# A branch gated on the last store but one, and ten small VectorE writes in an early wait

## The chip, the cores and the metric

The kernel runs on one core of one Trainium2 chip. The metric is the device time of one execution in microseconds, the median of several runs of the same program. A separate execution was recorded by the hardware profiler; all rows shown come from it. The core has five engines, each with its own queue of instructions: TensorE (PE; its weight loads are listed as PEld), VectorE (DVE), ScalarE (ACT), GpSimd (POOL) and SyncE (SP), which here only issues transfers and waits. A letter q behind the name (DVEq, SPq) stands for what the engine's sequencer does itself: waits on semaphores, branches, issue of transfers.

## The reference

Two stages over 4 batches, 8 heads, 768 positions, head width 64, in 8 blocks of 96 positions:

```
P = sort_net                                  # 4 x 8 x 8 x 8
5 times: P = exp(P - max(P, row)); P = P / rowsum; P = P / columnsum
k_sorted, v_sorted = P mixes the 8 blocks of k and of v
scores = scale * q_block @ k_sorted_block^T   # inside each block of 96
attn   = exp(scores - max) / sum ;  x = attn @ v_sorted
wq, wk = x @ w_q, x @ w_k
mixed  = (scale * wq @ wk^T) @ x
out    = relu(mixed) @ w_out                  # 4 x 768 x 512, float32
```

## The kernel before

Everything for the four batches is unrolled into one straight program. Its order is written out by hand in the string ORDER: each item is a unit (a letter for the kind, the batch, a number) with the engine or the PSUM bank that it uses, and the units are recorded in that order on the engines' queues. An engine executes its queue strictly in order.

At the start SyncE loads the sort matrix into `Pm` (L105). VectorE zeroes a padding column and the tile `fil` (L170, L171), then waits for the sort matrix and, with ScalarE for the exponentials, works through the five normalisations (`u_a` and `u_c`, L166 to L185). Meanwhile TensorE multiplies `fil` with itself 40 times, GpSimd prepares constants (`u_i`, with an affine select on `Lx` at L196) and issues the loads of q, k and v. From the sorted weights VectorE and GpSimd make the mixing matrices `M` (L234), and TensorE starts on the batches: sorting of k and v, transposes, scores, exponentials, products, and the second stage, all through the helper at L150 (matmul) and the copies at L154 (ScalarE) and L156 (VectorE).

The exponentials are taken without subtracting a maximum. GpSimd therefore tests all reciprocal sums (`test`, L457 to L461) and writes a flag `bad`; each of GpSimd, ScalarE, TensorE and VectorE loads it into a register (`flag`, L464). At the end of the program a branch on that register (L497) either enters a slow repair of the whole computation, some 450 instructions on VectorE, or jumps over it to the common end. With the inputs here it is always jumped over. Branch hints for TensorE and VectorE (`hint`) announce that the jump is likely. 

The outputs go through four buffers `ot` of two tiles each. For the last batch every tile of 128 rows is stored by a transfer of its own (`u_y`, L446), in the order 0, 1, 3, 4, 5, 2: tile 5 is the last but one, tile 2 the last. Buffer and half of a tile are given by `oslot`.

Ahead of the branch stands a gate (L492 to L496). VectorE writes one element into each half of the three buffers that the last batch uses; each such write has to wait until the stores out of that buffer have landed. Then VectorE writes `past`, and a tiny product on TensorE and a tiny copy on ScalarE read it, so that neither reaches its branch ahead of the gate. Behind the branch each engine raises a closing semaphore (L497). SyncE, which doesn't branch, goes through its closing waits (L598) one after the other: first the transfers, among them the last two stores in order, then the closing semaphores of VectorE, TensorE and ScalarE together with older transfers; then drains and a barrier of all engines end the program.

Of the kernel before, what the change touches and what calls it, by code (L numbers as in the profile page):

```python
# [56 lines left out]
def kernel(  # L57
# [11 lines left out]
    nc = tc.nc  # L69
# [18 lines left out]
    LAST = B - 1  # L88
# [9 lines left out]
    def tiles(name, n, shape, dtype=BF16):  # L98
        return [sb.tile(shape, dtype, name=f"{name}{i}") for i in range(n)]
# [23 lines left out]
    NOT = 4  # L123
    ot = tiles("ot", NOT, [P, 2, DM], FP32)
# [12 lines left out]
    past = sb.tile([1, 4], BF16, name="past")  # L137
# [5 lines left out]
    def rows(t):  # L143
        return t.unsqueeze(2).to_broadcast([BH, NB, NB])

    def cols(t):
        return t.unsqueeze(1).to_broadcast([BH, NB, NB])
# [20 lines left out]
    def u_c(b, n, e):  # L168
        if n == 0:
            nc.vector.memset(Pm[:, NB:NB + 1, :], 1e-9)  # L170
            nc.vector.memset(fil, 0.0)  # L171
            nc.vector.reduce_max(tmp, Pv, axis=AX.X)
            nc.vector.tensor_sub(Pv, Pv, rows(tmp))
            return
        nc.vector.reduce_sum(tmp, Pv, axis=AX.X)
        nc.vector.reciprocal(tmp, tmp)
        nc.vector.tensor_mul(Pv, Pv, rows(tmp))
        nc.vector.reduce_sum(tmp, Pm.rearrange("p i j -> p j i"), axis=AX.X)
        nc.vector.reciprocal(tmp, tmp)
        if n < 5:  # L180
            nc.vector.tensor_mul(Pv, Pv, cols(tmp))
            return
        nc.vector.tensor_mul(Pb.rearrange("p (i j) -> p i j", j=NB), Pv, cols(tmp))
        for a in range(2):
            nc.vector.transpose(PbT[:, a, :], Pb[:, a * BH:(a + 1) * BH])  # L185
# [249 lines left out]
    def oslot(b, n):  # L435
        return ot[(b * 3 + n // 2) % NOT][:, n % 2, :]
# [36 lines left out]
    for item in ORDER.split():  # L473
# [6 lines left out]
        kind, b, n, arg = UNIT.match(item).groups()  # L480
# [8 lines left out]
            fns[kind](b, num, arg)  # L489


    for n in range(3):  # L492
        nc.vector.memset(ot[(LAST * 3 + n) % NOT][0:1, :, 0:1], 0.0)  # L493
    nc.vector.memset(past[:, 0:1], 0.0)
    mm(PS[0:1, 0, 0:1], past[:, 0:1], past[:, 0:1])
    nc.scalar.copy(past[:, 1:2], past[:, 0:1])  # L496
# [106 lines left out]
```

## Time and profile before

| | |
|---|---|
| median of 3 runs | 107.63 us (107.57 to 107.66) |
| profiled execution, its own time | 107.97 us |
| its span, first to last instruction | 106.1 us |
| granted clock of TensorE | 0.998 |
| busy: PE, DVE, ACT, POOL | 93.6, 74.3, 70.1, 31.2 us |
| last store issued, landed | 101.14, 104.05 us |
| chain: PE, ACT, issue, DVE, DMA | 80%, 6%, 5%, 3%, 3% |

The profiled execution takes 1.9 us beside its span. Times in the rows count from the first instruction. A row of a timeline gives start, length, engine, line, operation, tiles and shapes, and in brackets how long the engine had been idle and what ended that. A row for one source line gives the smallest, median and largest duration in ns, then the first and the last start in us. A row of waits names who waited for whom: sum in us, count, longest. In the DMA view "q14 instruction" and "q8 instruction" are transfers that load instructions, not data (packets, MB, share of 16 engines over the window asked for).

### The profile page before, as it was taken

The page shows a single profiled execution, that of the slowest core. Times are in us where ns is not written, and L with a number is a line of the kernel's source. Part 1 is how long each engine was busy: PE and PEld are TensorE (multiplying, and loading weights), DVE is VectorE, ACT ScalarE, POOL GpSimd, SP SyncE. Part 2 cuts the span into 40 slices and gives each one's busy share as a digit, 9 for nine tenths or more (in the row PEclk, how much of TensorE's full clock was granted, in tenths as well). Part 3 has the DMA queues.
Part 4 walks back from the last instruction along what each step waited for, and adds up shares of the span by engine and source line. Part 5 has one row for each costly group of instructions (what it writes and reads, how often), then busy time and mean ns, then how long its engine had stood idle before and what let it go on. Part 6 is the DMA issues. An engine that isn't in the chain of part 4 may idle for free.

```text
span 106.1 us, 3639 instructions
## 1 busy us (share of the span) xinstructions
PE 93.6 (88%) x1550; PEld 65.7 (62%) x1557; DVE 74.3 (70%) x148; ACT 70.1 (66%) x102; POOL 31.2 (29%) x51
## 2 busy tenths in 40 slices
PE   5999999497897979899999999999999999999800
PEld 1334489485776866678968967686667556444400
DVE  1687789098895795788889887999777755637200
ACT  4101179769786879899779798689835447675510
POOL 5999099999237600000000000000059000000000
PEclk9999999999999999999999999999999999999999
DMA  0899999999999999999985474200039345198880
GB/s 3 84 203 203 203 204 208 200 204 205 206 203 204 190 202 204 204 204 205 207 163 134 115 208 106 76 6 0 0 120 380 139 198 204 60 402 326 296 302 14
DMA packets 18499, 18.55 MB, mean 175 GB/s; under 512 B 1840, under 2 KB 16560, under 8 KB 18480
## 3 DMA queue, kind: packets, MB, share of 16 engines
q0 software_dynamic: 14064, 10.09, 63.4%
q1 hardware_dynamic: 4416, 8.19, 22.1%
q8 instruction: 13, 0.21, 0.8%
q14 instruction: 6, 0.05, 0.1%
HBM read 20.19 MB, written 6.29 MB: 250 GB/s over the span
## 4 chain that ended last, share of the span: by engine, by line
PE 80%; ACT 6%; issue 5%; DVE 3%; DMA 3%; DVEq 0%; ACTq 0%
PE ps L150 80%; ACT E L340 3%; DMA out_dram<-ot 3%; DVE X L365 1%; ACT Vs L154 1%; DVE KT L156 1%; ACT XT L154 1%; ACT QT L154 1%; ACT ot L154 1%; DVE M L234 0%; DVE wk L156 0%; DVE fil L171 0%; DVE RS L363 0%; ACT past L496 0%; DVE ot L493 0%
## 5 line engine op out<-in xcount | busy, mean ns | idle before, releaser
L340 ACT ACTIVATE E<-ps 96x960 bf16<-96x960 f32 (+1 forms) x28 | 24.6, 906 | 3.1 <-PE ps L150 2.7
L150 PE MATMUL ps<-wo,mixT 128*128 128x512 bf16 (+1 forms) x93 | 22.2, 370 | 0.5 <-issue 0.2
L365 DVE TENSOR_TENSOR X<-ps,RS 96x896 bf16<-96x896 f32 (+1 forms) x20 | 20.1, 1007 | 0.7
L150 PEld LDWEIGHTS <-mixT 128*128 128x128 bf16 x100 | 8.9, 98 | 8.6 <-issue 0.2
L154 ACT COPY ot<-ps 128x512 f32<-128x512 f32 (+1 forms) x16 | 8.7, 560 | 8.1 <-PE ps L150 5.8
L457 POOL TENSOR_SCALAR ok<-RS 96x280 bf16<-96x280 f32 x1 | 0.9, 923 | 41.8 <-DVE RS L363 41.8
L150 PE MATMUL ps<-fil 128*128 128x512 bf16 x40 | 11.4, 458 | 1.3 <-DVE fil L171 1.3
L150 PE MATMUL ps<-VT,E 96*128 96x65 bf16 x256 | 11.2, 194 | 1.0 <-issue 0.6
L150 PEld LDWEIGHTS <-E 96*128 96x128 bf16 x256 | 9.8, 97 | 3.3 <-issue 1.1
L150 PE MATMUL ps<-QT,KT 64*128 64x96 bf16 x256 | 9.9, 204 | 1.7 <-issue 1.4
L234 POOL TENSOR_TENSOR M<-PTR,m_p 128x256 bf16<-128x256 bf16 x12 | 8.7, 744 | 7.0 <-PE ps L150 3.9
L156 DVE COPY ot<-ps 128x512 f32<-128x512 f32 x9 | 6.1, 690 | 6.5 <-PE ps L150 3.6
L150 PEld LDWEIGHTS <-KT 64*128 64x128 bf16 x256 | 6.9, 94 | 4.4 <-issue 3.2
L150 PEld LDWEIGHTS <-fil 128*128 128x128 bf16 x40 | 4.5, 115 | 7.8 <-issue 3.5
L154 ACT CAST KT<-ps 128x768 bf16<-128x768 f32 x10 | 7.7, 806 | 1.6 <-PE ps L150 1.5
L150 PE MATMUL ps<-idb,X 96*128 96x96 bf16 x128 | 7.5, 206 | 0.6 <-issue 0.6
L150 PE MATMUL ps<-M,Kn 128*64 128x128 bf16 x192 | 7.5, 221 | 0.3 <-issue 0.3
L156 DVE COPY QT<-ps 128x768 bf16<-128x768 bf16 x13 | 6.7, 550 | 1.5 <-PE ps L150 1.1
L426 ACT ACTIVATE mixT<-ps 128x1024 bf16<-128x1024 f32 x7 | 7.0, 1026 | 0.9 <-PE ps L150 0.6
L150 PEld LDWEIGHTS <-X 96*128 96x128 bf16 x128 | 6.2, 98 | 1.9 <-issue 0.9
L156 DVE COPY VT<-ps 96x1024 bf16<-96x1024 bf16 x7 | 4.8, 687 | 3.6 <-PE ps L150 2.9
L154 ACT COPY XT<-ps 128x768 bf16<-128x768 bf16 x6 | 4.8, 798 | 3.6 <-PE ps L150 3.6
(83 smaller groups left out, 156.8 us busy)
## 6 DMA issues: line engine op xcount, KB each, us to landing
out_dram<-ot SPq DMA_DIRECT2D x9, 512.0 KB, 2.8
Kn<-in_k_dram POOLq DMA_DIRECT2D x4, 768.0 KB, 13.1
Vn<-in_v_dram POOLq DMA_DIRECT2D x4, 768.0 KB, 15.2
Qn<-in_q_dram POOLq DMA_DIRECT2D x4, 768.0 KB, 15.3
VT<-Vs SPq DMA_DIRECT2D x12, 130.0 KB, 2.8
out_dram<-ot SPq DMA_DIRECT2D x6, 256.0 KB, 2.9
wo<-in_moe_w_out_dram POOLq DMA_DIRECT2D x1, 512.0 KB, 22.5
qD<-qkT SPq DMA_DIRECT2D x6, 48.0 KB, 2.7
```

Source lines behind the costliest of these rows:

```text
L150: nc.tensor.matmul(o, w, x, is_transpose=t, start=start, stop=stop, skip_group_check=True)
L154: nc.scalar.copy(o, i)
L156: nc.vector.tensor_copy(o, i)
L234: ENG[e].tensor_tensor(out=M[b % 2][:, h0:h1], in0=src[:, h0:h1].unsqueeze(2).to_broadcast([P, 2, SP, NB]), in1=m_p.unsqueeze(1).unsqueeze ...
L340: nc.scalar.activation(E[b % 2][:, n, 0:2 * w * BLK].rearrange("p (t a c) -> p a t c", a=2, c=BLK), PS[0:BLK, bank:bank + 2, 0:w * BLK].re ...
L365: nc.vector.tensor_mul(xo.rearrange("p (a t d) -> p a t d", a=2, d=D), ps[:, :, :, 0:D], rs.unsqueeze(3).to_broadcast([BLK, 2, w, D]))
L426: nc.scalar.activation(o, i, ACT.Relu)
L457: nc.gpsimd.tensor_scalar(out=okf, in0=rsf, scalar1=1e-30, scalar2=None, op0=ALU.is_ge)
```

## The change

Two edits. Ahead of the branch, one write replaces three: only the half buffer of tile 5 of the last batch (`oslot(LAST, 5)`) is written, so the gate waits for one store, the last but one. SyncE's closing waits are as before, so the program still ends only when all stores have landed. And in `u_c`, between the zeroing of `fil` and the first maximum over the sort matrix, VectorE writes the four elements of `past` ten times, each write behind the one before.

```diff
@@ u_c
         if n == 0:
             nc.vector.memset(Pm[:, NB:NB + 1, :], 1e-9)
             nc.vector.memset(fil, 0.0)
+            for _ in range(10):
+                nc.vector.memset(past, 0.0)
             nc.vector.reduce_max(tmp, Pv, axis=AX.X)
             nc.vector.tensor_sub(Pv, Pv, rows(tmp))
             return
@@ ahead of the branch
-    for n in range(3):
-        nc.vector.memset(ot[(LAST * 3 + n) % NOT][0:1, :, 0:1], 0.0)
+    nc.vector.memset(oslot(LAST, 5)[0:1, 0:1], 0.0)
     nc.vector.memset(past[:, 0:1], 0.0)
     mm(PS[0:1, 0, 0:1], past[:, 0:1], past[:, 0:1])
     nc.scalar.copy(past[:, 1:2], past[:, 0:1])
```

In the stream of VectorE's instructions the ten writes add ten places at the head. At the gate two writes and three separate waits go, five places. The other engines' streams keep their instructions and their order.

## The prediction

> **What bounds the kernel now.** I read the page's chain first, then the chain over the last six microseconds, then what SyncE's queue waits for there, then its final waits one by one.
>
> ```profile
> PE 80%; ACT 6%; issue 5%; DVE 3%; DMA 3%; DVEq 0%; ACTq 0%
> ...
> 100.52 0.59 ACT ot L154
> ...
> 101.14 2.92 DMA out_dram<-ot
> 104.05 0.03 issue
> 104.08 0.02 DVEq L493
> ...
> 104.52 0.19 ACT past L496
> ```
>
> Columns of the lower lines: start, length, what. TensorE sets the pace for 80% of the span, but it ends at about 100.5 us. Then the last copy and the last store (tile 2 of the last batch, lands at 104.05) run alone, and the gate at L493 starts only when that store has landed. The change touches this tail and the wait of VectorE at the very start, nothing between.
>
> ```profile
> SPq L598 <- DMA out_dram<-ot: 2.3, 2, 1.7
> SPq L598 <- DVEq L497: 0.8, 1, 0.8
> L598 SPq EVENT_SEMAPHORE  x1: 28/28/28, 103.5 to 103.5; - x1
> L598 SPq EVENT_SEMAPHORE  x4: 28/28/28, 104.1 to 104.2; - x4
> L598 SPq EVENT_SEMAPHORE  x1: 756/756/756, 104.3 to 104.3; - x1
> L598 SPq EVENT_SEMAPHORE  x2: 28/28/28, 105.1 to 105.2; - x2
> L598 SPq DRAIN  x2: 7/7/7, 105.2 to 105.3; - x2
> ```
>
> These are SyncE's closing waits, in order (length in ns, start in us). The one at 103.5 is freed by the last store but one (after 1.7 us of waiting), the next by the last store (after 2.3 - 1.7 = 0.6 us more). Four short ones follow, then one at 104.3 that lasts 756 ns instead of 28: it waits for VectorE's closing semaphore behind the branch, L497. Only then come two more waits, two drains and the common barrier to 106.1. So after the last store has landed, the way gate, branch, closing semaphore is the longer one, by 756 - 28 = 728 ns.
>
> ```profile
> 100.71 0.06 DVE L493 MEMSET ot<- 1x2 f32 x1 [0.80 <-DMA out_dram<-ot]
> 104.26 0.19 DVE L493 MEMSET ot<- 1x2 f32 x2 [3.49 <-DMA out_dram<-ot]
> 104.43 0.06 DVE L494 MEMSET past<- 1x1 bf16 x1
> L497 DVEq EVENT_SEMAPHORE  x1: 21/21/21, 105.0 to 105.0; - x1
> L497 ACTq EVENT_SEMAPHORE  x1: 17/17/17, 105.0 to 105.0; - x1
> L497 PEldq EVENT_SEMAPHORE  x1: 51/51/51, 105.0 to 105.0; - x1
> ```
>
> The three gate writes, the write of `past` that TensorE and ScalarE wait for, and the first instruction of each engine behind the branch.
>
> **The change, part by part: the gate.** Two of three writes go, and the one left waits for one store, the last but one (tile 5), instead of the last. What stood before it on VectorE's queue is done by 99.9 us, and nothing but `past` and the branch stands behind it. That store has landed at 103.45 to 103.5 (SyncE's row), so the gate opens 0.6 us earlier than at 104.05. From 104.05 to the write of `past` at 104.43 are 0.38 us for three queue waits and two writes; one wait and one write take about half, 0.1 to 0.2. So `past` is written at about 103.6, some 0.8 us earlier, and the three closing semaphores of 105.0 come at about 104.2. SyncE reaches its row for VectorE at 104.3. The wait of 756 ns then shrinks to the 28 ns of its neighbours: a gain of 0.73 us with a margin of 0.1 us. The two rows behind it wait for TensorE and ScalarE, whose semaphores move by the same 0.8 us, so they stay at 28 ns. Late next is the last store itself: SyncE still waits for its landing at 104.05, and no gate can buy more. The gain is bounded by 0 (the landing times of the two stores coincide, and the gate opens as late as now) and 0.73 us; I take 0.73, since the landings were 0.6 us apart and 0.5 would do.
>
> **The ten writes.** They stand behind the zeroing of `fil` and ahead of the first maximum over the sort matrix.
>
> ```profile
> 0.90 0.07 DVE L170 MEMSET Pm<- 32x8 f32 x1 [0.90 <-PEq L587]
> 0.99 0.27 DVE L171 MEMSET fil<- 128x256 uint32 x1
> 2.48 0.21 DVE L172 TENSOR_REDUCE tmp<-Pm 32x8 f32<-32x64 f32 x1 [1.21 <-DMA Pm<-in_sort_net_dram]
> ```
>
> VectorE is free from 1.26 to 2.48, waiting for a transfer that the writes don't touch. Each write waits for the one before. Their pitch: at least 0.03 us (104.39 to 104.43 in the chain, no wait between), at most 0.13 us (two gate writes, 0.19 us from the start of the first to the end of the second, less 0.06). I take 0.095, the pitch of the writes at 0.90 and 0.99: ten end at 1.26 + 0.95 = 2.21, hidden by the 1.21 us wait with 0.27 to spare. At 0.13 they end at 2.56, 0.08 late, and if that cover is gone the whole sort chain is late by as much; TensorE starts its first real product right after that chain. There is a second cover:
>
> ```profile
> 9.67 0.83 POOL L196 TENSOR_SCALAR_AFFINE_SELECT Lx<-Lx 32x512 bf16<-32x512 bf16 x1
> 9.82 0.72 DVE L181 TENSOR_TENSOR Pm<-Pm,tmp 32x64 f32<-32x64 f32 x1
> 8.04 0.21 DVE L181 TENSOR_TENSOR Pm<-Pm,tmp 32x64 f32<-32x64 f32 x1
> ```
>
> The fourth L181 takes 0.72 us instead of 0.21 and ends at 10.54, just behind GpSimd's at 10.50. If it is held by that, a chain late by 0.08 is back in step there. Cost taken: nothing; bound 0 to 0.08. [...]
>
> **The shift of the instruction blocks.** VectorE's stream gets ten instructions longer at its head and five shorter at the gate (two writes, three queue waits), so everything between stands ten places later and the branch five.
>
> ```profile
> L598 DVEq BRANCH_PREFETCH_HINT  x1: 51/51/51, 0.8 to 0.8; - x1
> q14 instruction: 1, 0.01, 4.0%
> q14 instruction: 1, 0.01, 3.9%
> DMA packets 0, 0.00 MB, mean 0 GB/s; under 512 B 0, under 2 KB 0, under 8 KB 0
> ```
>
> The second to fourth lines are the DMA view over 29.0 to 29.5, 100.7 to 101.2 and 104.4 to 105.1 us: one block of about 8 KB is loaded in each of the first two, none during the branch. Between the two loads VectorE executes some 126 instructions (by the program's order), so I read them as its next block, of 128, asked for when the stream enters a new one. At 100.7 it enters with the first gate write (100.71). The branch jumps some 450 instructions ahead, over the repair code, yet nothing is loaded at 104.4: the block at 100.7 must be the target's, announced by the hint. It has 3.7 us of gate wait to arrive. Shifted by ten, the entry falls on this copy:
>
> ```profile
> 95.33 0.69 DVE L156 COPY ot<-ps 128x512 f32<-128x512 f32 x1 [0.98 <-PE ps L150]
> ```
>
> Then the block is loaded at 94 to 97 us and is there long before the branch at about 103.6. Cost on the path: nothing. How much it would cost to be late is seen on TensorE:
>
> ```profile
> q8 instruction: 1, 0.02, 5.4%
> 26.42 0.27 PEld L150 LDWEIGHTS <-E 96*128 96x128 bf16 x7 [0.72 <-issue]
> ```
>
> Its block of 16 KB is in transfer from about 24.15 (DMA view of 24.1 to 25.2: 5.4% of 16 engines for 1.1 us, 0.95 us), and it stands still without any wait until 26.42: 2.3 us from load to first instruction. The other block load of VectorE moves with the shift too, from 29.1 to about 24 or 25, next to this one. Both lie on instruction queues; if they share an engine, TensorE's comes later by up to the 4.0% x 16 x 0.5 = 0.32 us of the small one, and TensorE is on the chain. Bound 0 to 0.32; I take 0, as one packet of 8 KB is little beside what the queues carry there anyway.
>
> **The sum.** Against the profiled execution (107.97 us, span 106.1): -0.73 + 0 + 0 + 0 = 107.24, span 105.35. The median of the runs shown is 0.34 lower than that execution, 107.63; the same 0.73 off gives 106.90, or 0.7% less. The branch, TensorE's stream and all stores are otherwise the same.
>
> **The rivals.**
> A. As forecast, 106.9 (106.65 to 107.05: the landings of the two stores may differ by 0.2 either way). Chance 0.70.
> B. The tail gains, but the moved block load or the late sort chain gives back 0.1 to 0.4 (0.32 + 0.08): 107.0 to 107.3. For it: TensorE starves for blocks at 26.42 with no slack. Against it: two small transfers on 16 engines seldom meet. Chance 0.10.
> C. The change doesn't do what it says: the two last stores land together in most runs, and the gate opens as late as before: 107.6. Against it: they land 0.6 us apart, and the rows below, of their issue, end 0.71 us apart (99.94 + 0.82 and 101.14 + 0.33). Chance 0.05.
>
> ```profile
> 99.94 0.82 SPq L446 DMA_DIRECT2D out_dram<-ot  x2
> 101.14 0.33 SPq L446 DMA_DIRECT2D out_dram<-ot  x1
> ```
>
> D. Slower: the target's block isn't there at the branch. One mechanism: if the hint only works for the entry next to the branch, the load at 95 brings the following block instead, and the branch at 103.6 must load its own. TensorE's row prices that: 2.3 us, or 2.3 - 0.64 = 1.7 with the smaller transfer. VectorE's closing semaphore then comes at 103.7 + 1.7 to 2.3 = 105.4 to 106.0 instead of 105.0, so 108.0 to 108.6. It decides from a delay of 0.85 us on; below that the gate's gain pays for it. Against it: the branch now stands further behind the entry, not nearer, and the hint is the same. Chance 0.10.
> [...]
> E. The blocks shift so that TensorE loses more than the tail gains: above 107.6. Chance 0.05.
>
> **How the numbers follow.** Two runs of this kernel can't be told apart within 0.2%, that is 0.22 us. A and B lie below 107.41: faster 0.80. C is the same: 0.05. D and E: slower 0.15. The range 106.65 to 107.3 holds A and B, 8 in 10. The time predicted is that of A.
>
> **What would show it.** In the profile after: SyncE's closing waits all at about 28 ns, with "DVEq" gone from what its queue waits for; one gate write at about 103.5; closing semaphores at about 104.2; the chain ending in the store's landing; ten writes of `past` between 1.2 and 2.3, the first maximum still at 2.48 and the first products of TensorE at the same times up to 57 us; an instruction block on VectorE's queue near 94 to 97 and none at 103.6. Wrong would be: a block load between 103.5 and 106 with a gap on VectorE behind it (D), TensorE's gap at 26.42 grown (B, E), or a last store but one that lands with the last (C).

## The result and the profile after

The changed kernel takes 106.33 us (median of 4 runs, 105.93 to 106.67) against 107.6 us before: a ratio of 0.9885, with an interval of 0.9846 to 0.9924. It is faster, as forecast, but by some 1.3 us and not by 0.7. 106.33 lies below the range of 106.65 to 107.3. The profiled execution of the changed kernel takes 106.25 us with a span of 104.3 us, against 107.97 and 106.1. So 1.73 us of it have to be found (spans of the trace, before rounding).

The chain of work that ended last, from the page of the changed kernel:

```profile
PE 72%; DVE 12%; issue 7%; ACT 5%; DMA 2%; DVEq 0%; ACTq 0%
```

The end of that chain (start, length, what):

```profile
99.38 0.38 ACT ot L154
99.76 0.02 issue
99.78 2.56 DMA out_dram<-ot
102.34 0.03 issue
...
102.45 0.06 DVE ot L494
...
102.58 0.19 ACT past L497
```

The chain now runs through the store of tile 5 (the last but one, landed at 102.34) into the gate at L494 and on to the end. The larger share of DVE does not come from the tail but from the first 12 us: in before TensorE's products of `fil` ran up to its first real product at 12.69 without a gap, so the chain followed them; in the changed kernel TensorE waited 0.22 us for the sort there (product at 12.63), so the chain follows the sort on VectorE.

**The tail is as predicted.** SyncE's closing waits and the first instruction of VectorE behind the branch, changed kernel:

```profile
L599 SPq EVENT_SEMAPHORE  x3: 28/28/28, 103.1 to 103.2; - x3
L599 SPq EVENT_SEMAPHORE  x4: 28/28/28, 103.3 to 103.4; - x4
L599 SPq DRAIN  x1: 7/7/7, 103.5 to 103.5; - x1
...
L498 DVEq EVENT_SEMAPHORE  x1: 21/21/21, 103.1 to 103.1; - x1
```

No wait is longer than 28 ns. VectorE's closing semaphore comes at 103.1, when SyncE asks for it at 103.3 it is there, and the row of 756 ns is gone. From the landing of the last store to the end it is now 1.295 us instead of 2.023: 0.73 of the 1.73 us.

**The last store lands sooner behind its issue.** The transfer view over 100.9 to 102.0 us (before) and 100.6 to 101.3 us (after), in which only the last store is issued. The last column is the time in us from issue to landing:

```profile
out_dram<-ot SPq DMA_DIRECT2D x1, 256.0 KB, 2.9
```

```profile
out_dram<-ot SPq DMA_DIRECT2D x1, 256.0 KB, 2.2
```

That is another 0.72 us (2.92 against 2.2), and nothing in the prediction stands for it. What the transfer engines do in the last 0.65 us before the landing tells where it comes from: 103.4 to 104.05 us before, 102.4 to 103.05 after.

```profile
DMA packets 3, 0.00 MB, mean 6 GB/s; under 512 B 1, under 2 KB 1, under 8 KB 3
```

```profile
DMA packets 42, 0.05 MB, mean 82 GB/s; under 512 B 16, under 2 KB 16, under 8 KB 42
```

Before, almost everything has landed by 103.4, and for 0.65 us the end waits for 3 packets. Every store of the last batch raises its semaphore 16 times in both traces (tile 2 in before from 103.17 to 104.05 us), and the chain has it landed with the 16th (104.05). I read each as the share of one of the 16 transfer engines that the view counts. The trace has the time of each:

| store (last batch) | 15 shares landed by | the 16th |
|---|---|---|
| before, tile 3 | 101.25 | 102.19 |
| before, tile 4 | 102.00 | 102.81 |
| before, tile 5 | 102.67 | 103.44 |
| before, tile 2, the last | 103.36 | 104.05 |
| after, tile 2, the last | 103.04 | 103.05 |

In before, one share lags from tile 3 on, by 0.94, 0.81, 0.77 and 0.69 us. The stores follow each other about every 0.7 us without a gap, so it makes up little of that. The trace doesn't name the engines; that it is the same one each time is inferred from this steady lag. The lag begins where VectorE's instruction block is loaded, at 100.80: the row of 3.9% on q14 that the prediction quotes. The engines are full of stores then, before over 100.6 to 101.3:

```profile
q1 hardware_dynamic: 133, 0.24, 96.3%
q14 instruction: 1, 0.01, 2.8%
```

In the changed kernel that load is seen over 90.9 to 91.8 us instead, when the transfer engines are idle otherwise:

```profile
DMA packets 1, 0.01 MB, mean 9 GB/s; under 512 B 0, under 2 KB 0, under 8 KB 0
...
q14 instruction: 1, 0.01, 3.7%
```

**The remaining 0.27 us lie at 20 us.** TensorE's weight loads there, before and then after:

```profile
20.47 0.09 PEld L150 LDWEIGHTS <-KT 64*128 64x128 bf16 x1 [1.54 <-issue]
```

```profile
20.20 0.09 PEld L150 LDWEIGHTS <-KT 64*128 64x128 bf16 x1 [1.33 <-issue]
```

TensorE stands still there for 1.54 and 1.33 us without a wait. I read this as the entry of a new block of its own instructions (16 KB on q8, loaded from 18.10 in before, from 17.81 after). After, it gets on 0.27 us sooner. This comes and goes from one execution to the next, with and without the change: the spans of the unchanged kernel's other executions lie nearly all at 105.5, 105.8 or 106.1 us, steps of about the same size.

### The profile page after: what moved, and what is told of

Read it like the earlier page. It is cut to its first block, busy times and chain, and to the rows that moved or that the text cites. A ratio compares the mean times of both kernels' runs of the same rounds, so it can differ in the third digit from the quotient of the medians.

```text
span 104.3 us, 3644 instructions
## 1 busy us (share of the span) xinstructions
PE 93.3 (89%) x1550; PEld 65.7 (63%) x1557; DVE 74.8 (72%) x156; ACT 70.1 (67%) x102; POOL 31.2 (30%) x51
## 4 chain that ended last, share of the span: by engine, by line
PE 72%; DVE 12%; issue 7%; ACT 5%; DMA 2%; DVEq 0%; ACTq 0%
PE ps L150 72%; DMA out_dram<-ot 2%; DVE Pm L183 1%; DVE tmp L180 1%; ACT Pm L166 1%; DVE Pm L179 1%; DVE X L367 1%; DVE tmp L177 1%; ACT Vs L154 1%; DVE tmp L181 1%; DVE tmp L178 1%; ACT E L342 1%; DVE KT L156 1%; ACT XT L154 1%; DVE past L173 1%
```

## The experiments

All kernels are compared with the kernel before, run beside them on the same chip (107.6 to 107.65 us). My theory after the result, as the expectations have it: two independent gains, the gate, and a stall of VectorE on entering a new block, which no longer delays the copy of tile 4. The rivals: the transfer of that block, not the stall, delays the stores; the writes themselves, or their place, do something else; or the gate alone moves everything. The experiments with the later entry and the held copy turned this round: it is the transfer.

| kernel | median us (range) | ratio and interval |
|---|---|---|
| changed kernel again | 106.06 (105.84 to 106.41) | 0.9853 (0.9829 to 0.9876) |
| gate alone | 106.86 (106.58 to 107.11) | 0.9931 (0.991 to 0.9951) |
| ten writes alone | 106.91 (106.58 to 107.13) | 0.9932 (0.9911 to 0.9953) |
| ten writes at 19 us | 106.2 (106.12 to 106.47) | 0.9881 (0.9861 to 0.9902) |
| one write | 106.27 (105.95 to 106.42) | 0.9857 (0.9834 to 0.988) |
| block entered one instruction later | 106.97 (106.59 to 107.13) | 0.9923 (0.9899 to 0.9947) |
| copy of tile 4 held back | 106.43 (106.15 to 106.64) | 0.9881 (0.9857 to 0.9906) |
| gate on tile 1 | 107.97 (107.71 to 108.74) | 1.0038 (1.0018 to 1.0058) |
| gate on tile 4 | 106.2 (105.98 to 106.52) | 0.9869 (0.9847 to 0.9891) |
| gate on tile 3 | 106.53 (106.24 to 106.76) | 0.9897 (0.9875 to 0.9919) |
| no hint for VectorE's branch | 108.46 (108.04 to 108.79) | 1.007 (1.0049 to 1.009) |

### The changed kernel again

No edit. 

> The changed kernel once more. Theory: three gains add up, the earlier gate (0.73 us), a stall of about 0.38 us on VectorE that no longer falls on the copy of tile 4 (and lets the last stores land earlier), and 0.2 to 0.3 us early in the kernel: 106.2 to 106.5 us. Rival, the early part is a difference between single executions: 106.4 to 106.7, and the early times in this trace are those of before.

Its profiled execution takes 106.41 us (span 104.6), 0.3 more than the first one; its first gap on TensorE ends at 20.20 as in the first, and it loses that again at the next gap, near 32.5 us. From there on it runs in step with before (ScalarE's last copy starts at 100.52 in both), so this pair is the clean comparison: 1.45 us of span (104.62 against 106.07), of which 0.73 is the closing wait and 0.72 the landing (2.2 us behind its issue here too). The median of 106.06 us lies below both ranges that I had expected.

### Each part alone

The gate alone:

```diff
-            for _ in range(10):
-                nc.vector.memset(past, 0.0)
```

> The gate of the change, without the ten writes. Theory: only the way from gate to closing semaphores gets shorter, 0.73 us, so 106.8 to 107.0 us; the copy of tile 4 still starts 0.42 us after its last wait has ended, and the last store still takes 2.9 us. Rival, the gate gives all: 106.3. Rival, the branch now comes too soon after the block entry and waits for the target's block: 107.3 or more, with a gap behind the branch on VectorE.

The writes alone:

```diff
-    nc.vector.memset(oslot(LAST, 5)[0:1, 0:1], 0.0)
+    for n in range(3):
+        nc.vector.memset(ot[(LAST * 3 + n) % NOT][0:1, :, 0:1], 0.0)
```

> The ten writes, with the gate of before. Theory: the stall leaves the copy of tile 4, so its store is issued about 0.38 us earlier and the last store lands 0.4 to 0.7 us earlier, while 728 ns of SyncE's closing wait stay: 106.9 to 107.2 us. Rival, the writes only delay or do nothing: 107.5 to 107.8. Rival, the whole gain is one of blocks: 106.3.

The last store in the transfer view, with the gate alone, and with the writes alone:

```profile
out_dram<-ot SPq DMA_DIRECT2D x1, 256.0 KB, 2.9
```

```profile
out_dram<-ot SPq DMA_DIRECT2D x1, 256.0 KB, 2.2
```

SyncE's closing waits from 103.5 us on, with the gate alone (from 103.2) and with the writes alone:

```profile
L597 SPq EVENT_SEMAPHORE  x5: 28/28/28, 103.2 to 104.0; - x5
L597 SPq EVENT_SEMAPHORE  x4: 28/28/28, 104.0 to 104.2; - x4
```

```profile
L600 SPq EVENT_SEMAPHORE  x2: 28/395/762, 103.5 to 103.6; - x2
```

The two gains are cleanly apart. The gate alone shortens the closing wait (28 ns) and leaves the late landing (2.9 us; the 16th share at 103.78 against 103.08 for the 15th, block load at 100.53). The writes alone bring the landing (2.2 us, block load at 91.5) and leave the wait of 762 ns. By the medians they bring 0.74 and 0.69 us; both together brought 1.27 and 1.54 in the two measurements of the changed kernel. Both times are as expected, but the stall that I gave for the second is not its cause, as shown below.

### Is it the writes, their place, or their number?

The ten writes moved to an idle time of VectorE near 19 us (`r0.10` is a new unit of ten writes):

```diff
-                 ... q0.2@D S0.6@0
+                 ... q0.2@D r0.10@D S0.6@0
-            for _ in range(10):
-                nc.vector.memset(past, 0.0)
```

> The change, but the ten writes stand in VectorE's idle time near 19 us instead of at the start. The later block entry falls on the same instruction as in the changed kernel. Theory, place does not matter but for the shift: 106.2 to 106.6, the late copies as in the changed kernel. Rival, the early 0.27 us came from the writes at the start: 106.5 to 106.7 with TensorE's first gap ending near 20.5 us again. Rival, writes here delay the copies that TensorE waits for: above 106.7.

One write in place of ten:

```diff
-            for _ in range(10):
+            for _ in range(1):
                 nc.vector.memset(past, 0.0)
```

> The changed gate with one write instead of ten. VectorE's block entry then falls one instruction earlier than without writes: on the wait ahead of the copy of tile 4, which lasts 1.56 us anyway. Theory, the entry stalls VectorE for 0.38 us wherever it falls, and costs time only where VectorE is awaited: the copy of tile 4 starts within 0.05 us of the end of its wait, and the time is 106.1 to 106.6 us, as with ten writes. Rival, the ten writes act in another way than by the place of the entry: 106.8 to 107.0 as without writes. Rival, the block's load next to the last stores is what costs: the copy is early, but the last store still takes 2.9 us, 106.5 to 106.8.

Both are as fast as the changed kernel: 106.2 and 106.27 us. With the writes at 19 us the block load is at 91.29 and the rest as in the changed kernel, so that they stand in the wait for the sort matrix does not matter. With one write the load comes at 98.29 us, while the stores are only starting. Over 98.0 to 98.6:

```profile
q1 hardware_dynamic: 33, 0.07, 29.9%
q14 instruction: 1, 0.01, 4.4%
```

The transfer engines have time to spare (29.9%, against 96.3% around 100.8 us in before), and the shares of the last store land together. The first store of the batch has a share that is 0.13 us late (100.05 against 99.92), and by tile 3 nothing of that is left. So one place of shift is enough, and what counts here is whether the load meets full transfer engines.

### The load or the stall?

VectorE also stands still itself, at what I read as its entry into the block. Its timeline, before and then after:

```profile
97.13 0.69 DVE L156 COPY ot<-ps 128x512 f32<-128x512 f32 x1 [0.24 <-PE ps L150]
99.22 0.69 DVE L156 COPY ot<-ps 128x512 f32<-128x512 f32 x1 [1.40 <-PE ps L150]
```

```profile
96.85 0.69 DVE L156 COPY ot<-ps 128x512 f32<-128x512 f32 x1 [0.24 <-PE ps L150]
98.56 0.69 DVE L156 COPY ot<-ps 128x512 f32<-128x512 f32 x1 [1.02 <-PE ps L150]
```

In before the copy of tile 4 starts 0.42 us after its wait for TensorE has ended, in the changed kernel 0.04 after: 0.38 us of stall at the entry, and a later copy makes a later store. Which of the two is the 0.72? First, both transposes of the sort in one instruction and no writes, which leaves VectorE's queue one instruction shorter and, by my count, puts the entry just behind that copy:

```diff
-            for _ in range(10):
-                nc.vector.memset(past, 0.0)
...
-        for a in range(2):
-            nc.vector.transpose(PbT[:, a, :], Pb[:, a * BH:(a + 1) * BH])
+        nc.vector.transpose(PbT.rearrange("p a h -> p (a h)"), Pb)
```

> The changed gate, no writes, and the two transposes of the sorted weights made in one instruction (the same values): VectorE's stream is one instruction shorter, so the block entry falls just behind the copy of tile 4, on the wait of the gate. Theory: the copy is no longer late, the block's load still comes near 100.5 to 101, among the last stores, and the branch follows only three instructions behind: 106.1 to 106.6 if the load harms no store and is there in time. Rival, the load among the stores costs some 0.3 us: 106.4 to 106.9 with a last store of 2.5 us or more. Rival, the target's block comes late: a gap behind the branch, 107 or more.

VectorE's timeline, then the transfer view over 100.6 to 101.3, the last store, and 103.4 to 104.05 us, all of this kernel:

```profile
98.84 0.69 DVE L156 COPY ot<-ps 128x512 f32<-128x512 f32 x1 [1.02 <-PE ps L150]
```

```profile
q1 hardware_dynamic: 140, 0.26, 100.4%
q14 instruction: 1, 0.01, 2.8%
...
out_dram<-ot SPq DMA_DIRECT2D x1, 256.0 KB, 2.9
...
DMA packets 3, 0.00 MB, mean 6 GB/s; under 512 B 1, under 2 KB 1, under 8 KB 3
```

The copy is on time (98.84, as in the repeat of the changed kernel), the load is still at 100.80, and the loss is all there: 2.9 us to the landing, 3 packets at the end, the last share at 104.05 with 15 landed by 103.30. The load costs it, without the stall. My theory, by which this load would harm no store (106.1 to 106.6), is out; the rival had 106.4 to 106.9, and 106.97 is just above.

Second, the stall without the load among the stores: the copy of tile 4 held back by three one-column copies in the changed kernel.

```diff
+        if b == LAST and n == 4:
+            for _ in range(3):
+                nc.vector.tensor_copy(oslot(b, n)[:, 0:1], PS[:, bank, 0:1])
```

> The changed kernel, with three copies of one column ahead of VectorE's copy of tile 4, each waiting for the one before (the values stay the same): they hold that copy back by 0.3 to 0.6 us, as the stall did, while the block entry stays where the ten writes put it. Theory, the last stores queue behind each other, so a late tile 4 alone makes the last store land late, by more than the copy's own delay: 106.7 to 107.0, last store near 2.9 us. Rival, about half of the landing gain came from the block's load having left the stores: 106.4 to 106.7, last store 2.4 to 2.6 us.

```profile
98.83 0.54 DVE L443 COPY ot<-ps 128x1 f32<-128x1 f32 x3 [1.02 <-PE ps L150]
99.41 0.69 DVE L156 COPY ot<-ps 128x512 f32<-128x512 f32 x1
```

The copy starts 0.57 us later than in the repeat, and the last store lands 0.23 us later (103.56). Even a delay larger than the stall thus costs a third of what the load costs: the stores queue at the transfer engines anyway, which they keep 96.8% busy here over 100.9 to 102.0 us. In before the 15th share lands at 103.36, and in the repeat of the changed kernel at 103.31, so the stall is worth about 0.05 us there. The 106.7 to 107.0 us of the stall theory did not come; 106.43 us and 2.4 us to the landing are the rival's.

### How far can the gate go?

The gate set on an earlier store, tile 1, 4 or 3 in place of 5:

```diff
-    nc.vector.memset(oslot(LAST, 5)[0:1, 0:1], 0.0)
+    nc.vector.memset(oslot(LAST, 1)[0:1, 0:1], 0.0)
```

> The changed kernel, with the gate's one write on tile 1 instead of tile 5: its store lands some 2 us before the last. Theory, behind the last landing SyncE's own waits set the end, so no earlier gate buys anything: 106.1 to 106.5, the same as the changed kernel within 0.2%. Rival, the gate still sets part of the end: 105.8 or less.

> The changed kernel with the gate on tile 4, the store before the last but one, landed at 101.7 us in the changed kernel's trace. The branch is then taken at about 101.9, the engines enter new blocks at about 102.4 and ask for the next ones at about 103.0, just as the last store lands (103.05). Theory, loads that hit the tail of the last store hold up one of 16 transfer engines each: between 106.1 (they miss it) and 107.0 (they hit it). Rival, the loss with the gate on tile 1 came from something else than the loads behind the branch: 107.5 or more here as well.

> The changed kernel with the gate on tile 3, landed at 101.0 us. The branch comes at about 101.2, the loads behind it at about 102.2 to 102.4, in the middle of the last store. Theory: up to three transfer engines are held up for 0.7 to 1.9 us, 107.0 to 108.0, as with the gate on tile 1. Rival, only the very early gate does harm: 106.1 to 106.6.

On tile 1 the kernel is slower than before, which neither the theory nor the rival had. Its transfer view over 102.0 to 102.3, over 103.1 to 104.95, and for the last store:

```profile
q1 hardware_dynamic: 51, 0.10, 87.5%
q8 instruction: 1, 0.02, 28.2%
q14 instruction: 2, 0.02, 12.9%
...
DMA packets 17, 0.03 MB, mean 16 GB/s; under 512 B 3, under 2 KB 3, under 8 KB 17
...
out_dram<-ot SPq DMA_DIRECT2D x1, 256.0 KB, 4.1
```

The branch is taken at 100.4 to 100.5 us, and 1.6 us later three instruction blocks are loaded (102.06, 102.14, 102.17) into the last store: 13 of its shares land by 103.02, the other three at 103.74, 104.13 and 104.94, the last 4.1 us after its issue and not 2.2. Three loads, three late shares: this fits a load holding up one engine. Three such loads follow the branch in before too, at 105.56 to 105.67. In the changed kernel they come at 103.62 to 103.73, when all has landed. On tile 3 they come at 102.41 to 102.49 and cost 0.5 us (2.7 us to the landing). That is less than the 0.7 to 1.9 I expected, and 106.53 lies in the rival's range, though the loads do harm. On tile 4 they come at 102.98 to 103.06, at the very landing, and cost nothing (2.2 us); 106.2 us cannot be told from the changed kernel.

### The hint

VectorE's announcement of the branch left out of the changed kernel's ORDER:

```diff
-... y2.1@S hintD H3.0@4
+... y2.1@S H3.0@4
```

> The changed kernel without VectorE's branch hint. If the hint is what brings the target's block, VectorE has to load it at the branch, 102.5 us: its closing semaphore comes 1.2 us or more later than 103.1, a block load shows near 102.7 and holds up the last store by about 0.7 us besides: 107.0 to 107.9. If the block comes without the hint, 106.1 to 106.5.

SyncE's closing wait at 103.3, and behind the branch at L498:

```profile
L599 SPq EVENT_SEMAPHORE  x1: 2574/2574/2574, 103.3 to 103.3; - x1
...
L498 DVEq COMPARE_BRANCH  x1: 72/72/72, 102.5 to 102.5; - x1
...
L498 PEldq EVENT_SEMAPHORE  x1: 51/51/51, 103.1 to 103.1; - x1
L498 DVEq EVENT_SEMAPHORE  x1: 21/21/21, 105.8 to 105.8; - x1
```

VectorE branches at 102.5 and executes its next instruction at 105.83: 3.34 us, against 0.6 with the hint, and TensorE, which keeps its hint, is there at 103.1. A first instruction block is loaded at 103.53, 2.3 us ahead of that instruction. The last store still lands as in the changed kernel (2.2 us), since the loads come after it; I had expected one near 102.7 that delays it, and at most 107.9 us. With the hint no load shows between the branch at 102.48 and the next instruction at 103.08. So I read that in this kernel the hint is what has the target's block there in time.

## Why the prediction was right and wrong

**The gate, -0.73: right.** Measured 0.74 us alone, and the waits are at 28 ns as forecast. The gate write comes at 102.45 and not at 103.6, since the landings themselves moved.

**"No gate can buy more": right, but incomplete.** The gate on tile 4 buys nothing more. That an earlier gate costs (0.5 us on tile 3, 1.9 us on tile 1, both at the last landing) I had not seen, because I took the branch for free of transfers.

**The ten writes, 0: right.** Their pitch is 0.115 us, between my bounds and above the 0.095 I took. The opening of the changed kernel on VectorE:

```profile
0.99 0.27 DVE L171 MEMSET fil<- 128x256 uint32 x1
1.20 1.11 DVE L173 MEMSET past<- 1x2 uint32 x10
2.33 0.21 DVE L174 TENSOR_REDUCE tmp<-Pm 32x8 f32<-32x64 f32 x1
```

The first maximum starts at 2.33 us, 0.02 us after the sort matrix has landed (2.31). With the writes elsewhere (2.28, 2.30) and in before (2.45, 2.48) it is 0.02 us too, so the writes delay nothing. The 0.15 us against before is the earlier landing, and 0.06 of it is left at TensorE's first product (12.63 against 12.69). The fourth L181, now L183, is stretched again (0.80 against 0.72 us) and takes up most of the difference, as the second cover has it, here for a chain that is early. It ends 0.04 us behind GpSimd's select in both kernels (10.54 and 10.50 in before, 10.47 and 10.43 after); whether GpSimd holds it was not tried.

**The shift of the instruction blocks, "cost on the path: nothing": wrong, and this is the step that failed.** The load did move off 100.8, as I said, and the branch found its block there (no load between it at 102.48 and the next instruction at 103.08). But I asked only what it costs to have the block late, and not what the block's transfer did where it had stood, and I took all stores to be "otherwise the same". I had its row (3.9% of 16 engines over 100.7 to 101.2, in the middle of the last stores) and did not price it; of the other load I wrote that one packet of 8 KB is little. By the late share (0.69 to 0.94 us in before) I read that it held up one of the 16 engines that the last stores needed, and each store landed with its slowest share. The term is -0.7 us, measured alone at 0.69. The bound that I gave the step, a cost of 0 to 0.32 for the other load, had no gain in it. With -0.7 in its place the sum is 106.90 - 0.7 = 106.2, between the two medians of 106.06 and 106.33.

**"They land 0.6 us apart": right for before, but for a reason I did not see.** The 0.61 us are between two late shares. The 15th shares are 0.69 apart there, and in the changed kernel the landings are 0.71 apart.

**Entry with the first gate write (100.71), load at 94 to 97: wrong in place.** The entry was at the copy of tile 4 (98.8 to 99.2), and the load starts behind the entry: 2.0 us in before, 1.09 us in the changed kernel, where the same 0.4 us of standstill shows at 90.02 to 90.45. So ten places moved the load to 91.1. VectorE's first block load went from 29.1 to 20.3 and not to 24 or 25; no cost of it is seen.

**The rivals.** A had the gate right, but its 106.65 to 107.05 misses 106.33, and no rival had a last store that lands sooner. B is out (its load moved and cost nothing), C is out (0.74 us). D does not happen, and the kernel without the hint shows that its price was too low: without the block VectorE is late by 3.34 - 0.6 = 2.7 us and not 1.7 to 2.3. That its time of 108.46 lies in D's 108.0 to 108.6 is luck: that range was reckoned without the 0.7 us of the landing. E is out.

**Open.** The load itself takes 2.8% x 16 x 0.7 = 0.31 us of an engine, and the share was late by 0.94 us at first and by 0.69 at the end; why it is more than twice was not tried. Which engine a load uses the traces do not tell. The 0.27 us at 20 us vary by execution: the early start of TensorE (20.20) is there in all traces but those of before, the later entry and the held copy. That it also appears with the gate alone, which changes nothing that early, speaks against the change as its cause; what decides it was not settled.

## What to carry to other kernels

In this kernel an instruction load in the middle of stores made one share of them late by 0.7 to 0.9 us, as if both shared a transfer engine. Look up in the transfer view when such loads come, and if one falls among back-to-back stores at the end, shift the program by an instruction or more so that it falls into a quiet time. Here each store landed with the last of its 16 shares, so I read a few last packets in an otherwise empty view (3 over 0.65 us in before, 42 after) as a sign of one engine that was held up. Let the last branch go only so early that the loads behind it do not meet the last store: meeting it cost 0.5 us with the gate on tile 3 and 1.9 us with the gate on tile 1.

## What the runs showed of the hardware beyond that

- With an 8 KB instruction load among the last stores (engines 96.3% busy with them) the last store landed 2.92 us behind its issue, without it 2.2; with three loads behind a branch (two of 8 KB, one of 16 KB) 4.1 us.
- VectorE's queue stood still for 0.4 us at what I read as the entry of a new block: 98.80 to 99.22 in before, ahead of a copy, and 90.02 to 90.45 in the changed kernel, ahead of a wait.
- Further blocks were loaded from 1.1 us (before, the changed kernel) to 1.6 us (gate on tile 1) after VectorE's taken branch on: in the changed kernel at 103.62 to 103.73, in the last microsecond of the program.
- Ten writes of four elements behind one another had a pitch of 0.115 us on VectorE in the changed kernel.
